# Block attention and its feed-forward: token chunks of 384 instead of 512, one PSUM bank moved, another pace of the half units

## The chip, the cores and the metric

One core of a Trainium2 chip runs the whole program in one launch. The metric is the device time of one execution in microseconds (us); lower is better. Its engines run side by side, each in the order of its own queue, and wait for each other on semaphores: TensorE (PE, with its weight loads shown as PEld) multiplies into PSUM, VectorE (DVE) and ScalarE (ACT) read PSUM and SBUF, GpSimd (POOL) works in SBUF, and SyncE (SP) issues every DMA of this kernel.

## What is computed

```python
# q, k, v: (8, 8, 576, 64) f32;  w_in: (512, 2048);  w_out: (2048, 512)
scores = np.matmul(q, k.transpose(0, 1, 3, 2)) / np.sqrt(64)
mask = block_i >= block_j                       # blocks of 64 positions
attn = exp(where(mask, scores, -1e9) - max)     # rows divided by their sum + 1e-9
x = np.matmul(attn, v)                          # (8, 8, 576, 64)
x = x.transpose(0, 2, 1, 3).reshape(4608, 512)  # heads side by side: 4608 tokens
h = x @ w_in
g = np.where(h >= 1, h, np.where(h <= -1, 0.0, (h + 1) ** 2 / 4))
out = g @ w_out                                 # (4608, 512) f32
```

## The kernel before

**Number format.** The products run in a rounded 32-bit format, with each operand held as a high and a low part, and three products of parts stand for one (high by high, low by high, high by low). The weights are taken apart on the chip: `prepare_weights` works through 64 pieces of 128 by 256, each with one DMA in, three DVE instructions, three on ACT and two on POOL. The parts of `w_in` stay in SBUF (`wih`, `wil`); those of `w_out` go to DRAM (`wo_split`) and come back 512 KB at a time.

**Attention.** A batch has four pairs of heads, so there are 32 pairs. `attention_steps` is a generator that lays out each pair in eight steps (a step ends at a `yield`), 258 steps in all: scores, softmax, transposes of the probabilities, products with `v`. From the second batch on, probabilities hop through a DMA (line 250) before they are transposed. Every result in PSUM takes a bank from `work_bank` (lines 80 to 85), which hands out the `ps_w` banks in turn; a bank comes free when ACT and DVE have read it. While `banks["free"]` holds, every second request gets a bank of `ps_o` instead.

**Feed-forward.** It goes by chunks of `TCH` = 512 tokens (9 chunks) and, in a chunk, by 16 slices of 128 hidden columns. One slice is one unit, made of two half units. `ffn_in` (lines 763 to 788) runs 12 matmuls of 512 columns into the one bank `ph`, then ACT L779, DVE L780 and DVE L783 turn it into `t` (L783 is the last to read `ph`), ACT L784 makes `gh`, POOL L785 `gl`, and SP L787 loads `wo`, of which there are two buffers. `ffn_out` (lines 790 to 811) runs 8 matmuls at L794 and 4 at L799, one set of 3 for each of the `NTT` = 4 groups of 128 tokens in the chunk, into 4 `po` banks; after the last slice the banks are copied out and stored. `feed_forward` yields after each half unit, and `ffn_out` of a slice comes behind `ffn_in` of the next.

**PSUM.** Eight banks: 3 `ps_w`, 1 `ph`, 4 `po` (lines 74 to 76).

**The interleaving** (lines 830 to 855). From step `START` = 36 (the fourth step of the fifth pair) one half unit of the feed-forward follows each attention step, and `want` sets how many weight pieces are converted by then: all 64 during the first 24 or so of these steps. When the attention has ended, the half units that are left run alone. The x of the attention goes to a ring of `RING` = 1536 tokens. The layout in the source is a priority; a scheduler at build time settles the order on each engine from its own estimates, so a few instructions stand earlier or later than their step.

## Time and profile before

| what | value |
| --- | --- |
| median of 3 runs | 1270.7 us (1269.4 to 1272.47) |
| the profiled execution: its time, its span | 1269.69 us, 1267.9 us |
| PE busy, share of the span | 1200.1 us, 95% |
| PEld, DVE, ACT, POOL busy | 998.8, 887.0, 703.2, 394.6 us |
| mean granted TensorE clock | 0.981 of full speed |
| matmuls | 6280, of which 3456 belong to the feed-forward |

The span is the time from the first to the last instruction of the profiled execution; the 1.8 us beside it lie around the program. Busy times of different engines overlap. Matmuls are pipelined and their ends are modelled, so the busy time of PE says little by itself: the distance from the start of one matmul to the start of the next is what a matmul takes in a stream. The trace falls into four stages, told apart by the steps of the source: attention with some weight pieces (steps 0 to 35, up to 113.6 us), attention with the rest of the weights and the first feed-forward half units (steps 36 to 67, 113.6 to 290 us, called the converting stage), attention with feed-forward (steps 68 to 257, 290 to 1081.9 us, the overlapped stage), and feed-forward alone (the tail, 1081.9 to 1268 us).

### The profile page before, as it was taken

The numbers are of one execution on the slowest core, as the hardware profiler recorded it, in microseconds if no ns is written. First come the engines' busy times: TensorE is split into PE (matmuls) and PEld (weight loads), VectorE is DVE, ScalarE is ACT, GpSimd is POOL, SyncE is SP. The second block draws the span as 40 slices with busy tenths as digits, with TensorE's granted clock in tenths as the row PEclk, the third lists the DMA queues.
The fourth block names the chain that finished last, engine by engine and source line by source line (L and its number), as shares of the span: only waits on it lengthen the run. The fifth ranks groups of instructions, "written<-read, shape, count | busy, mean of one in ns | idle before, by whom it ended". The sixth has DMA issues, their size and how long they took to land.

```text
span 1267.9 us, 20253 instructions
## 1 busy us (share of the span) xinstructions
PE 1200.1 (95%) x6280; PEld 998.8 (79%) x6280; DVE 887.0 (70%) x2188; ACT 703.2 (55%) x1827; POOL 394.6 (31%) x430
## 2 busy tenths in 40 slices
PE   5888889899999999999999999999999999999998
PEld 4666667678888888888888888888888888888886
DVE  8898877758777777777777777787777777322222
ACT  5787656646566655665656655566556555222222
POOL 3555655522222222222222222222222222222222
PEclk9888988999999999999999999999999999999999
DMA  5566666667888655555554655465556433422432
GB/s 158 167 176 215 203 228 197 217 198 237 260 273 266 215 162 158 154 175 163 156 162 145 187 157 152 138 189 153 160 154 190 137 128 118 132 87 98 133 100 100
DMA packets 185259, 215.43 MB, mean 170 GB/s; under 512 B 113840, under 2 KB 132272, under 8 KB 184384
## 3 DMA queue, kind: packets, MB, share of 16 engines
q1 hardware_dynamic: 185152, 214.14, 54.9%
q8 instruction: 50, 0.82, 0.3%
q14 instruction: 57, 0.47, 0.1%
HBM read 134.74 MB, written 31.98 MB: 131 GB/s over the span
## 4 chain that ended last, share of the span: by engine, by line
PE 69%; DVE 16%; ACT 6%; issue 5%; DMA 1%; POOL 1%; SPq 1%; ACTq 0%; POOLq 0%; DVEq 0%
PE ph L770 29%; PE po L794 15%; PE po L799 7%; PE ps_av L591 7%; PE ps_s L482 4%; ACT pr L509 3%; PE ps_s L485 3%; DVE t L780 2%; PE ps_t L552 2%; DVE t L783 2%; ACT t L779 2%; DVE pb L547 2%; DVE nm L505 2%; DVE sm L491 1%; DVE pr L515 1%
## 5 line engine op out<-in xcount | busy, mean ns | idle before, releaser
L785 POOL TENSOR_TENSOR gl<-t,gh 128x512 fp32r<-128x512 f32 x144 | 187.5, 1302 | 510.2 <-ACT gh L784 333.2
L794 PE MATMUL po<-wo,gh 128*128 128x512 f32 x1152 | 296.1, 397 | 0.5 <-DMA wo<-wo_split 0.3
L794 PEld LDWEIGHTS po<-wo,gh 128*128 128x128 f32 x1152 | 212.5, 189 | 44.5 <-DMA wo<-wo_split 0.7
L770 PE MATMUL ph<-xh,wih 128*128 128x512 f32 x576 | 232.9, 404 | 1.6 <-DVE t L783 1.6
L770 PE MATMUL ph<-xh,wil 128*128 128x512 f32 x576 | 228.8, 397 | 0.0
L770 PE MATMUL ph<-xl,wih 128*128 128x512 f32 x576 | 227.8, 396 | 0.5 <-DVE xl L627 0.5
L780 DVE SCALAR_TENSOR_TENSOR t<-t 128x512 f32<-128x512 f32 x144 | 101.5, 705 | 168.0 <-ACT t L779 165.2
L779 ACT ACTIVATE t<-ph 128x512 f32<-128x512 f32 x144 | 85.9, 597 | 173.8 <-PE ph L770 173.8
L509 ACT ACTIVATE pr<-ps_s,nm 128x128 f32<-128x128 f32 (+3 forms) x256 | 134.1, 527 | 60.5 <-DVE nm L505 58.4
L784 ACT CAST gh<-t 128x512 fp32r<-128x512 f32 x144 | 89.5, 621 | 120.3 <-DVE t L783 120.0
L799 PE MATMUL po<-wo,gl 128*128 128x512 f32 x576 | 155.6, 392 | 0.0
L482 PE MATMUL ps_s<-ka,qa 68*128 68x288 f32 (+4 forms) x384 | 135.3, 367 | 15.0 <-ACT pr L509 5.4
L379 POOL TENSOR_TENSOR vsr<-vn,vsr 128x256 fp32r<-128x256 f32 (+1 forms) x96 | 55.2, 576 | 246.2 <-ACT vsr L378 244.6
L770 PEld LDWEIGHTS ph<-xh,wil 128*128 128x128 f32 x576 | 109.5, 190 | 23.8
L770 PEld LDWEIGHTS ph<-xh,wih 128*128 128x128 f32 x576 | 109.8, 191 | 21.7 <-DVE t L783 2.3
L799 PEld LDWEIGHTS po<-wo,gl 128*128 128x128 f32 x576 | 108.7, 189 | 23.1
L505 DVE TENSOR_REDUCE nm<-ps_s 128x1 f32<-128x128 f32 (+3 forms) x256 | 118.8, 482 | 10.4 <-PE ps_s L485 9.4
L770 PEld LDWEIGHTS ph<-xl,wih 128*128 128x128 f32 x576 | 109.7, 190 | 20.5 <-DVE xl L627 0.9
L485 PE MATMUL ps_s<-kb,qb 128*128 128x288 f32 (+4 forms) x384 | 121.1, 322 | 0.0
L515 DVE TENSOR_SCALAR pr<-pr,sm 128x128 f32<-128x128 f32 (+3 forms) x256 | 107.3, 440 | 5.4
L783 DVE TENSOR_TENSOR t<-ph,t 128x512 f32<-128x512 f32 x144 | 98.7, 686 | 2.2
L491 DVE TENSOR_SCALAR sm<-sm 128x1 f32<-128x1 f32 (+1 forms) x224 | 52.0, 232 | 68.3 <-ACT pr L509 65.7
(111 smaller groups left out, 1871.4 us busy)
## 6 DMA issues: line engine op xcount, KB each, us to landing
wo<-wo_split SPq DMA_DIRECT2D x144, 512.0 KB, 3.5
prr<-pr SPq DMA_DIRECT2D x96, 192.0 KB, 2.5
prr<-pr SPq DMA_DIRECT2D x72, 256.0 KB, 2.8
out_dram<-ob SPq DMA_DIRECT2D x36, 256.0 KB, 2.9
bits<-in_moe_w_in_dram SPq DMA_DIRECT2D x32, 256.0 KB, 3.5
bits<-in_moe_w_out_dram SPq DMA_DIRECT2D x32, 256.0 KB, 3.0
wo_split<-ws SPq DMA_DIRECT2D x16, 512.0 KB, 2.9
qa<-qb SPq DMA_DIRECT2D x63, 128.0 KB, 2.4
```

The source lines that it names most:

```text
L482: nc.tensor.matmul(ps, qa[:KA, j, c0 : c0 + P], ka[:KA, j, k0 : k0 + n], start=first, stop=False)
L485: nc.tensor.matmul(ps, qb[:, j, c0 : c0 + P], kb[:, j, k0 : k0 + n], start=False, stop=last)
L505: nc.vector.tensor_reduce(out=nm[:, i : i + 1], in_=ps[:, cs], axis=AX.X, op=ALU.max, negate=True)
L509: nc.scalar.activation(pr[:, cs], ps[:, cs], AF.Exp, bias=nm[:, i : i + 1], scale=1.0, accum_out=sm[:, i : i + 1],)
L515: nc.vector.tensor_scalar_mul(pr[:, cs], pr[:, cs], sm[:, i : i + 1])
L770: nc.tensor.matmul(ph, w[:, cc, fs], x[:, cc, xs], start=(cc == 0 and i == 0), stop=(cc == NCC - 1 and i == 2),)
L779: nc.scalar.activation(t_, ph, AF.Relu, bias=0.5, scale=0.5)
L780: nc.vector.scalar_tensor_tensor(out=t_, in0=t_, scalar=1.0, in1=t_, op0=ALU.min, op1=ALU.mult)
L783: nc.vector.tensor_tensor(out=t_, in0=ph, in1=t_, op=ALU.max)
L785: nc.gpsimd.tensor_tensor(out=gl, in0=t_, in1=gh.bitcast(F32), op=ALU.subtract)
L794: nc.tensor.matmul(po[tt], gh[:, ts_], wo[:, w, :], start=(fc == 0 and w == 0), stop=False)
L799: nc.tensor.matmul(po[tt], gl[:, ts_], wo[:, 0, :], start=False, stop=fc == NFC - 1)
```

## The change

Chunks are 384 tokens: 12 chunks, `NTT` = 3, so that `po` takes three banks and `ps_w`, by `bufs=7 - NTT`, four. The matmuls of `ffn_in` have 384 columns instead of 512, and a unit has 12 of them as before; `ffn_out` has 9 matmuls of 512 columns instead of 12. The ring keeps 1536 tokens (4 chunks). Lines that used `TCH` as the width of a bank now use `BANK` = 512, with the same value as before. The pace: for the first 32 steps from `START` one half unit a step, as before, and then three half units for two steps (`due`). The number of weight pieces for each of these steps stays.

```diff
-    TCH = 512
+    TCH = 384
+    BANK = 512
...
-    RING = 3 * TCH
+    RING = 4 * TCH
...
-    ps_w = ctx.enter_context(tc.tile_pool(name="ps_w", bufs=3, space=bass.MemoryType.PSUM))
+    ps_w = ctx.enter_context(tc.tile_pool(name="ps_w", bufs=7 - NTT, space=bass.MemoryType.PSUM))
...
-            dst = pool.tile([P, TCH], F32R, tag=tag, name="prr")
+            dst = pool.tile([P, BANK], F32R, tag=tag, name="prr")
...
-        ph = ps_h.tile([P, 512], F32, tag="ph", name="ph")
+        ph = ps_h.tile([P, TCH], F32, tag="ph", name="ph")
...
-    converted = 0
+    converted = done = 0
...
         else:
+
+            due = i - START + 1 + max(0, i - START + 1 - 2 * NFC) // 2
             want = max(
-                EARLY + (i - START + 1) * (NFC // GROUP * PART - EARLY) // (2 * NFC - 4 * GROUP),
-                ((i - START) // (2 * GROUP) + 1) * PART,
+                EARLY + due * (NFC // GROUP * PART - EARLY) // (2 * NFC - 4 * GROUP),
+                ((due - 1) // (2 * GROUP) + 1) * PART,
             )
...
         if i >= START:
             banks["free"] = False
-            next(ffn_steps, None)
+            for _ in range(due - done):
+                next(ffn_steps, None)
+            done = due
```

## Rows read from the trace of the kernel before

**Rows 1.** Timeline, DVE: line 539 of the fifth and ninth pair (start, length).

```profile
113.76 0.16 DVE L539 TENSOR_TENSOR sm<-sm 128x1 f32<-128x1 f32 x1
...
289.54 0.16 DVE L539 TENSOR_TENSOR sm<-sm 128x1 f32<-128x1 f32 x1 [1.14 <-ACT pr L535]
```

**Rows 2.** Stretches: length, busy time by engine, granted clock, DMA share, GB/s.

```profile
113.60:290.00 176.40, 157.06 (x732) 122.71 (x733) 128.03 (x314) 102.93 (x289) 85.38 (x102) 0.92 0.67 212
290.00:1081.90 791.90, 777.78 (x4317) 659.32 (x4314) 608.88 (x1494) 473.63 (x1218) 209.17 (x218) 1.00 0.57 175
1081.90:1268.00 186.10, 180.90 (x796) 148.90 (x794) 49.68 (x73) 43.67 (x73) 43.99 (x34) 0.99 0.33 108
```

**Rows 3.** Waits of PE and PEld in the overlapped stage: total us, times, longest.

```profile
PE ps_qk L442 <- DVE x L614: 8.9, 23, 0.4
PE ps_s L482 <- ACT pr L509: 5.2, 17, 0.3
...
PEld ps_qk L442 <- PE ps_s L485: 15.7, 23, 0.7
PEld ps_s L482 <- ACT pr L509: 10.1, 23, 0.5
```

**Rows 4.** Timeline, one unit of the tail: start, length, engine, line.

```profile
1207.50 0.40 PE L770 MATMUL ph<-xh,wil 128*128 128x512 f32 x1
...
1207.73 1.98 PE L794 MATMUL po<-wo,gh 128*128 128x512 f32 x8
...
1209.35 0.69 DVE L783 TENSOR_TENSOR t<-ph,t 128x512 f32<-128x512 f32 x1
...
1210.46 0.39 PE L770 MATMUL ph<-xh,wih 128*128 128x512 f32 x1
```

**Rows 5.** Timeline, PE: a 384-column matmul and its successor.

```profile
728.78 0.34 PE L485 MATMUL ps_s<-kb,qb 128*128 128x384 f32 x1
728.96 0.39 PE L770 MATMUL ph<-xh,wih 128*128 128x512 f32 x1
```

**Rows 6.** Timeline, PE: the first two matmuls of a half unit behind attention.

```profile
712.91 0.47 PE L770 MATMUL ph<-xh,wih 128*128 128x512 f32 x1
...
713.22 0.39 PE L770 MATMUL ph<-xl,wih 128*128 128x512 f32 x1
```

**Rows 7.** Groups by line and shape: count, busy us, mean ns, idle before.

```profile
L779 ACT ACTIVATE t<-ph 128x512 f32<-128x512 f32 x144 | 85.9, 597 | 173.8 <-PE ph L770 173.8
...
L547 DVE TENSOR_TENSOR pb<-ps_t,pb 128x384 fp32r<-128x384 f32 x48 | 26.6, 554 | 0.7
...
L545 ACT CAST pb<-ps_t 128x384 fp32r<-128x384 f32 x48 | 22.8, 475 | 0.0
```

**Rows 8.** DMA issues of `wo`, and SP's waits in the overlapped stage.

```profile
wo<-wo_split SPq DMA_DIRECT2D x144, 512.0 KB, 3.5
...
SPq L787 <- PE ps_t L552: 169.3, 65, 6.4
```

**Rows 9.** Chain of waits in the converting stage: shares of its 176.4 us.

```profile
by line: PE ph L770 15.4%; issue 11.1%; PE ps_av L591 10.4%; POOL work L183 5.5%; PE po L794 4.6%; DVE t L780 3.4%; DVE work L177 3.1%; DVE work L171 3.0%; ACT pr L509 2.7%; DMA prs<-pr 2.5%; PE po L799 2.5%; DVE work L174 2.3%; DMA bits<-i
```

**Rows 10.** Converting stage, lines 770, 794 and 799 alone: length, PE, PEld, clock, DMA.

```profile
113.60:290.00 176.40, 56.65 (x192) 38.63 (x192) 0.92 0.67 212
...
113.60:290.00 176.40, 33.97 (x120) 22.67 (x120) 0.92 0.67 212
...
113.60:290.00 176.40, 16.97 (x60) 11.83 (x60) 0.92 0.67 212
```

**Rows 11.** Waits of PE in the converting stage for banks that scores hold.

```profile
PE ps_av L591 <- ACT pr L509: 3.7, 3, 2.2
PE ps_t L552 <- ACT pr L509: 3.0, 2, 1.9
```

**Rows 12.** Timeline, PE: two neighbours in a slow stretch of the converting stage.

```profile
117.16 0.63 PE L770 MATMUL ph<-xl,wih 128*128 128x512 f32 x1
117.58 0.63 PE L770 MATMUL ph<-xh,wil 128*128 128x512 f32 x1
```

More of the change, by code (lines that the diff above doesn't have):

```diff
@@ L234, in as_float32r @@
                 spare["of"] = [t_[:, :NTL, :, :].rearrange("p t h d -> p (t h d)") for t_ in vsr]
-                spare["of"].append(att1.tile([P, S], F32R, tag="x32", name="prs")[:, :TCH])
+                spare["of"].append(att1.tile([P, S], F32R, tag="x32", name="prs")[:, :BANK])
                 spare["end"] = att1.tile([P, G0 + P], F32R, tag="pa11", name="pre")[:, :BLK]
@@ L238, in as_float32r @@
             spare["n"] += 1
-            if src.shape[1] > TCH:
+            if src.shape[1] > BANK:
                 moved.append(spare["end"])
             for i, dst in enumerate(moved):
-                n = min(TCH, src.shape[1] - i * TCH)
-                nc.sync.dma_start(dst[:, :n].bitcast(F32), src[:, i * TCH : i * TCH + n])
+                n = min(BANK, src.shape[1] - i * BANK)
+                nc.sync.dma_start(dst[:, :n].bitcast(F32), src[:, i * BANK : i * BANK + n])
             return moved
         moved = []
-        for c0 in range(0, src.shape[1], TCH):
-            n = min(TCH, src.shape[1] - c0)
+        for c0 in range(0, src.shape[1], BANK):
+            n = min(BANK, src.shape[1] - c0)
             pool, tag = ((conv, "bits"), (conv2, "work"))[c0 > 0]
-            dst = pool.tile([P, TCH], F32R, tag=tag, name="prr")
+            dst = pool.tile([P, BANK], F32R, tag=tag, name="prr")
             nc.sync.dma_start(dst[:, :n].bitcast(F32), src[:, c0 : c0 + n])
@@ L549, in transposed @@
         def transposed(self, out, parts, c0, n):
-            src = parts[c0 // TCH][:, c0 % TCH : c0 % TCH + n] if self.hop else parts[0][:, c0 : c0 + n]
+            src = parts[c0 // BANK][:, c0 % BANK : c0 % BANK + n] if self.hop else parts[0][:, c0 : c0 + n]
             if self.hop:
```

## The prediction

> **What bounds the kernel now.** The page comes first: PE is busy 95% of the span, but its matmul ends are modelled, so the next question is where PE stands still. The busy times by stretch answer it. I cut the trace where the fourth step of the fifth and of the ninth pair ends (line 539 runs once a pair) [rows 1], because the source starts the feed-forward at the first and has converted all weights by the second. In the overlapped stage PE is busy 777.8 of 791.9 us at full clock; in the tail all but the start and the end [rows 2]. So both are bound by PE, and DVE, the next, has 608.9 us to do there. In the converting stage PE is busy 157.1 of 176.4 us at a clock of 0.92, DVE 128.0 [rows 2], and the chain of waits runs over PE, DVE, POOL and DMA by turns [rows 9]: no engine bounds it alone.
>
> The view of the waits says what PE's 14.1 idle us in the overlapped stage are: 8.9 before L442 and 5.2 before L482 [rows 3]. Both are waits for a bank. L442 (`turned_last`) needs the bank that `attn_v_first` took three requests earlier, which DVE L614 empties; the 512-column scores need the one whose exponentials (ACT L509) end late. The weight loads show the same waits as 15.7 and 10.1 us [rows 3], longer because modelled matmul ends cover part of them.
>
> **The change, part by part.** *A matmul.* [...] A half unit of either kind costs 2.73 us now. Afterwards `ffn_in` costs 12 x 0.174 = 2.09 and `ffn_out` 9 x 0.2275 = 2.05.
>
> [...]
>
> *Where the half units lie.* The converting stage has 32 steps, the overlapped one 190. Half units in them and in the tail, before: 32 (17 `ffn_in`), 190, 66. After: 32, 285 (222 + 95 = 317 by the last step), 67. PE time:
> - converting: 87.4 before; 17 x 2.09 + 15 x 2.05 = 66.3 after: -21.1.
> - overlapped: 518.7 before; 142 x 2.09 + 143 x 2.05 = 590.0 after: +71.3.
> - tail: 180.2 before; 33 x 2.09 + 34 x 2.05 = 138.7 after: -41.5.
>
> Together +8.7: the kernel gets no less matmul work, it gets it at other places. In the tail and the overlapped stage, where PE is the bound, these are times. In the converting stage -21.1 is only an offer.
>
> *The fourth bank.* With it L442 needs the bank of the scores before, whose exponentials come two requests earlier, and the 512-column scores that of an earlier transpose. So the two waits go: 14.1 us by the idle time, 25.8 by the loads [rows 3]. I take -18, nearer to the idle time, as the transposes behind them then wait for probabilities instead, now and then. The scheduler's other choices could take all of it (bound 0).
>
> *Starts.* A half unit that begins behind attention has 0.31 from its first to its second matmul [rows 6], 0.08 over the pitch. The 95 half units more are 47 units more: +3.8 (0 to 4).
>
> *The single `ph` bank.* `ffn_in` waits until L783 has read `ph`. In the tail this is 1207.50 to 1210.04, 2.54 us from the start of the last matmul, and the next `ffn_in` starts at 1210.46 [rows 4]. At 384 columns ACT's part shrinks from 597 to about 475 ns and DVE's two from 0.69 to about 0.55 each [rows 4, 7], the last matmul by 0.05: 2.54 - 0.12 - 0.27 - 0.05 = 2.10, and PE is back after 0.17 + 2.05 = 2.22. The margin falls from 0.42 to 0.12, so the first load may come late: +1 in the tail (0 to 5). In the overlapped stage two in three `ffn_in` will have but one attention step between them, the shortest with five transposes and two 512-column matmuls, at least 0.7 us by their streams: 2.9 against 2.1 plus what ACT and DVE do in between. I take +1 (0 to 20).
>
> *Other engines.* 48 units more of five instructions on ACT, DVE and POOL are shorter each; DVE's two make 192 x 1.10 = 211 against 200 us, covered by its idle 183 us in the overlapped stage. The `wo` loads go from 144 to 192. Each waits on SP for a buffer, and the DMA hops of the probabilities queue behind it; SP stands there 169 us of 792 [rows 8]. A buffer's turn, in the tail 2.09 + 2.05 + 2.09 = 6.2 us, still covers the 3.5 to landing, so I take nothing; if that cover went, a hop would be late and a transpose would wait as in the third rival. Before step 36 the banks are still seven, so nothing moves.
>
> *The converting stage.* What does it give back of 21.1? At least what leaves the chain: L770 15.4%, L794 and L799 7.1%, L780 3.4% of 176.4 us [rows 9], times 0.234, 0.25 and 0.20: 6.4 + 3.1 + 1.2 = 11. At most what leaves PE's busy time, where a part runs at 1.2 GHz: 56.65 x 0.234 + 50.94 x 0.25 = 26 [rows 10], and the waits for score banks, 6.7 [rows 11]: 33. I take -21: PE is busy 89% of the stage, which draws to the upper end, and the pieces' chain over DVE and POOL, unchanged, to the lower.
>
> *Sum.* Overlapped +71.3 - 18 + 3.8 + 1 = +58.1; tail -41.5 + 1 = -40.5; converting -21. Together -3.4 on the span of 1267.9, so 1264.5, and with the 1.8 us around it 1266.3. The profiled run lies 1.0 under the median, so 1267 for the median.
>
> **The rivals.** *The converting stage does not give it back* (slower). The balance of the other stages is +17.6, so below 17.6 the change loses. For it: the weight pieces keep their number a step, and POOL and DVE work on them stands in the chain beside 11.1% "issue" [rows 9]. A PE with less to do may also run slower: neighbours at 117.16 are 0.42 apart, 1.2 GHz, and the stage's clock is 0.92 [rows 2, 12]. Against: the feed-forward's own lines hold 26% of that chain. With 6 to 10 us given back: 1278 to 1282.
>
> [...]
>
> *The converting stage is PE's* (faster): 33 back, and 20 or more for the banks: 1250 to 1257. For it: 89% busy. Against: DVE, 5 us lighter, would be busy 86% of the 143 us left.
>
> *`ph` becomes the wait.* If the chain L779, L780, L783 takes over 2.9 us because attention stands in ACT's and DVE's queues, 95 of the 142 `ffn_in` wait, by 0.2 us 19 us: 1286. Against: two steps' slack is gone only for two in three.
>
> *The waits stay* (the change does not do what it says): the bank was not the last condition, only the latest semaphore. The 18 us are not gained: 1285. Against: L442 reads `qk`, which the source loads six steps earlier.
>
> *Weight loads bind at 384 columns*: 148.90 us for 794 loads in the tail [rows 2], 0.19 each, against 0.174: 2304 x 0.016 = 37 us, 1304. Against: [rows 5].
>
> **How the numbers follow.** Chances: forecast 0.42 (its own range 1260 to 1274), no giving back 0.23, PE's stage 0.17, `ph` 0.09, waits stay 0.06, loads 0.03. The range 1250 to 1284 leaves out a third of PE's stage, half of the two cases at 1285 and the loads, 0.16 in all. A measurement here can tell about 0.2%, 2.5 us, from no change. Faster by more: 0.27 of the forecast's 0.42 and all of PE's stage, 0.44. Within: 0.12 of the forecast and the upper edge of no giving back, 0.17. Slower: the rest, 0.39.
>
> **What would show it.** In the trace after: 384-column neighbours at L770 0.174 apart (0.19: loads); no wait before L442 and L482 in the overlapped stage; that stage at some 850 us, the tail at 146, the converting stage at 155. A converting stage over 160 us makes the forecast wrong; a wait of L770 on L783 there or in the tail points to `ph`.

## The result, and the profile after

The changed kernel takes 1273.49 us (median of 20 runs, 1270.51 to 1276.81) against 1267.99 for the kernel before, timed beside it (20 runs): a ratio of 1.0044, with a 95% interval of 1.0034 to 1.0054. It is slower by more than the 0.2% that can be told apart, where I had forecast 1267 and a gain as the likeliest. The profiled execution has a span of 1271.5 us; that of before had 1267.9, a difference of 3.6. The medians lie 5.5 apart; most of the rest is that the profiled execution of before, 1269.69 us, lies 1.7 above the median of its 20 runs.

The stretches of the changed kernel, cut at the same events as [rows 1] (line 539 is now 540): length, busy time and count of PE, PEld, DVE, ACT and POOL, granted clock, DMA share, GB/s.

```profile
0.00:113.10 113.10, 83.89 (x443) 68.30 (x444) 99.77 (x311) 82.93 (x250) 56.00 (x76) 0.92 0.58 172
113.10:281.20 168.10, 134.53 (x699) 111.77 (x698) 123.18 (x313) 100.78 (x289) 80.19 (x102) 0.94 0.69 216
281.20:1125.40 844.20, 842.26 (x5015) 766.91 (x5014) 659.54 (x1595) 493.82 (x1309) 229.60 (x266) 1.00 0.63 196
1125.40:1271.50 146.10, 141.15 (x706) 124.03 (x704) 41.32 (x73) 35.79 (x71) 35.38 (x35) 1.00 0.41 135
```

Cut at exactly those events, the stages of before [rows 1, 2] are 113.8, 175.7, 792.4 and 186.0 us; its converting stage, so cut:

```profile
113.80:289.50 175.70, 156.36 (x730) 122.10 (x730) 127.45 (x310) 102.72 (x287) 85.38 (x102) 0.92 0.66 211
```

| stage | before | after | change | forecast |
| --- | --- | --- | --- | --- |
| first (steps 0 to 35) | 113.8 | 113.1 | -0.7 | 0 |
| converting | 175.7 | 168.1 | -7.6 | -21 |
| overlapped | 792.4 | 844.2 | +51.8 | +58.1 |
| tail | 186.0 | 146.1 | -39.9 | -40.5 |
| span | 1267.9 | 1271.5 | +3.6 | -3.4 |

**The overlapped stage and the tail came nearly as worked out.** The waits of PE and PEld in the overlapped stage (total, times, longest) answer [rows 3]:

```profile
PE po L795 <- DMA wo<-wo_split: 0.9, 1, 0.9
PE ph L771 <- DVE t L784: 0.9, 4, 0.3
...
PEld ph L771 <- DVE t L784: 10.8, 31, 0.7
```

The waits before L442 and L482 (now 443 and 483) are gone; PE is busy 842.26 of 844.20 us. A unit of the tail answers [rows 4] (start, length, engine, line):

```profile
1201.51 0.33 PE L771 MATMUL ph<-xl,wih 128*128 128x384 f32 x1
...
1203.24 0.34 PE L771 MATMUL ph<-xh,wil 128*128 128x384 f32 x1
...
1203.41 1.55 PE L795 MATMUL po<-wo,gh 128*128 128x512 f32 x6
...
1204.79 0.56 DVE L784 TENSOR_TENSOR t<-ph,t 128x384 f32<-128x384 f32 x1
...
1205.48 0.37 PE L771 MATMUL ph<-xh,wih 128*128 128x384 f32 x1
```

From 1201.51 to 1203.41 lie eleven distances of 384-column matmuls, 0.173 each (0.174 had been worked out). From the start of the last one to the end of L784, which frees `ph`, pass 2.11 us, and PE is back 2.24 us after that start: the forecast had 2.10 and 2.22. The first load of the next `ffn_in` waits a moment in 32 units (6.3 us in all), the matmuls themselves don't.

**The converting stage is where the forecast failed.** PE's busy time there, cut at the same events, was 156.36 us before and is 134.53 now, 21.8 less, about the 21.1 that the half units had promised. But its idle time went from 19.3 to 33.6. What PE waits for now (first fence), and what ACT and DVE wait for (second):

```profile
PE ph L771 <- DVE t L784: 17.4, 8, 4.4
PE ps_t L553 <- DMA prs<-pr: 6.5, 5, 1.8
PE ps_t L553 <- DMA vsr<-pr: 2.9, 6, 0.9
```

```profile
ACT wih L186 <- POOL work L184: 20.3, 16, 3.2
...
ACT ws L186 <- POOL work L184: 9.4, 11, 1.5
...
DVE t L781 <- ACT t L780: 11.8, 8, 2.5
```

The waits for score banks of [rows 11] are not among PE's larger ones any more. In their place PE stands 17.4 us at `ffn_in`, because `ph` is not free: L781 waits 11.8 us for ACT's L780, and ACT in its turn stands 29.7 us at the copy of a weight piece (L186), which needs POOL's addition (L184). That stop of ACT is not new: in the kernel before it was 27.1 us (15.4 and 11.7). What is new is that PE, with less to do, reaches `ph` before it is free (1.6 us of such waits before). The transposes wait for probabilities that hop through a DMA. The chain of waits of this stage, to be held against [rows 9]:

```profile
by line: issue 12.6%; POOL work L184 6.8%; DMA prs<-pr 5.8%; PE ph L771 4.3%; DVE work L172 4.1%; DVE work L178 4.0%; PE ps_av L592 3.7%; DVE pr L516 3.6%; DVE work L175 3.6%; DMA prr<-pr 3.5%; PE po L795 3.0%; ACT pr L510 2.9%; DVE t L781 
```

L770's share was 15.4%, that of L794 and L799 7.1%; now L771 has 4.3% and L795 3.0%. POOL's and DVE's lines of the pieces (L184, L172, L178, L175) add up to 18.5%, and "issue" and two hops of probabilities to 21.9%. Most of the feed-forward's matmuls left the chain, and the chain became only a little shorter. By pairs, the four of the stage took 39.5, 46.7, 49.1 and 40.4 us before, and 33.2, 40.3, 50.1 and 44.6 after: the first two gave back 12.7 us, the last two took 5.2 of it again.

### The profile page after: what moved, and what is told of

It reads as the page before. It is cut to its first block, busy times and chain, and to the rows that moved or that the text cites. A ratio compares the mean times of both kernels' runs of the same rounds, so it can differ in the third digit from the quotient of the medians.

```text
span 1271.5 us, 21767 instructions
## 1 busy us (share of the span) xinstructions
PE 1201.8 (95%) x6856; PEld 1071.0 (84%) x6856; DVE 923.8 (73%) x2290; ACT 713.3 (56%) x1917; POOL 401.2 (32%) x478
## 4 chain that ended last, share of the span: by engine, by line
PE 77%; DVE 11%; DMA 3%; ACT 3%; issue 2%; POOL 1%; SPq 1%; DVEq 0%; ACTq 0%; POOLq 0%
PE ph L771 29%; PE po L795 19%; PE po L800 9%; PE ps_av L592 7%; PE ps_s L483 4%; PE ps_t L553 3%; PE ps_s L486 3%; DVE pr L516 2%; DVE nm L506 1%; PE ps_qk L402 1%; DVE work L172 1%; DVE t L781 1%; DVE work L175 1%; POOL work L184 1%; ACT pr L510 1%
## 5 line engine op out<-in xcount | busy, mean ns | idle before, releaser
L786 POOL TENSOR_TENSOR gl<-t,gh 128x384 fp32r<-128x384 f32 x192 | 195.6, 1019 | 655.0 <-ACT gh L785 478.5
L795 PE MATMUL po<-wo,gh 128*128 128x512 f32 x1152 | 305.7, 399 | 2.5 <-DMA wo<-wo_split 2.2
L771 PE MATMUL ph<-xh,wih 128*128 128x384 f32 x768 | 267.7, 349 | 19.5 <-DVE t L784 18.4
L771 PE MATMUL ph<-xh,wil 128*128 128x384 f32 x768 | 259.9, 338 | 0.0
L771 PE MATMUL ph<-xl,wih 128*128 128x384 f32 x768 | 259.4, 338 | 0.0
L781 DVE SCALAR_TENSOR_TENSOR t<-t 128x384 f32<-128x384 f32 x192 | 130.0, 677 | 152.5 <-ACT t L780 148.7
L795 PEld LDWEIGHTS po<-wo,gh 128*128 128x128 f32 x1152 | 208.6, 189 | 38.1 <-DMA wo<-wo_split 1.7
L785 ACT CAST gh<-t 128x384 fp32r<-128x384 f32 x192 | 98.6, 513 | 207.6 <-DVE t L784 206.5
L771 PEld LDWEIGHTS ph<-xh,wih 128*128 128x128 f32 x768 | 145.6, 190 | 42.6 <-DVE t L784 37.3
L780 ACT ACTIVATE t<-ph 128x384 f32<-128x384 f32 x192 | 94.0, 490 | 135.1 <-PE ph L771 133.7
L800 PE MATMUL po<-wo,gl 128*128 128x512 f32 x576 | 164.1, 392 | 0.0
L771 PEld LDWEIGHTS ph<-xl,wih 128*128 128x128 f32 x768 | 145.6, 190 | 3.0
L771 PEld LDWEIGHTS ph<-xh,wil 128*128 128x128 f32 x768 | 145.3, 189 | 0.2
L506 DVE TENSOR_REDUCE nm<-ps_s 128x1 f32<-128x128 f32 (+3 forms) x256 | 119.0, 484 | 21.8 <-PE ps_s L486 20.8
L800 PEld LDWEIGHTS po<-wo,gl 128*128 128x128 f32 x576 | 108.2, 188 | 23.5
L784 DVE TENSOR_TENSOR t<-ph,t 128x384 f32<-128x384 f32 x192 | 105.8, 551 | 2.3
L553 PEld LDWEIGHTS ps_t<-ident_r,prr 128*128 128x128 f32 x600 | 68.9, 139 | 14.6 <-ACT t L780 1.5
L548 DVE TENSOR_TENSOR pb<-ps_t,pb 128x512 fp32r<-128x512 f32 (+1 forms) x120 | 76.0, 634 | 3.3 <-ACT pb L546 1.8
```

Source lines behind the costliest of these rows:

```text
L506: nc.vector.tensor_reduce(out=nm[:, i : i + 1], in_=ps[:, cs], axis=AX.X, op=ALU.max, negate=True)
L553: nc.tensor.transpose(out.bitcast(F32R), src, ident_r)
L771: nc.tensor.matmul(ph, w[:, cc, fs], x[:, cc, xs], start=(cc == 0 and i == 0), stop=(cc == NCC - 1 and i == 2),)
L781: nc.vector.scalar_tensor_tensor(out=t_, in0=t_, scalar=1.0, in1=t_, op0=ALU.min, op1=ALU.mult)
L784: nc.vector.tensor_tensor(out=t_, in0=ph, in1=t_, op=ALU.max)
L786: nc.gpsimd.tensor_tensor(out=gl, in0=t_, in1=gh.bitcast(F32), op=ALU.subtract)
```

## The experiments

The question of the first runs: are the weight pieces what holds the converting stage, and by which engine; and is the fourth bank, or `ph`, what the change is worth elsewhere? All stage lengths below are cut at the same events as above, and in each run the stages that the edit doesn't touch came out within 3 us of the kernel that it starts from, unless the text says so. A stage length comes from one profiled execution, and in the converting stage the granted clock lay anywhere from 0.86 to 0.99 in these runs, so a few us there say little by themselves. Where a kernel was run four times or more, an estimate from its median helps: the median less the 1.8 us around the span and less the overlapped stage and the tail of its trace leaves the first two stages together, 287.8 us before and 281.4 after, 6.4 apart. The kernels of 4, 5 and 7 and the first two of 6 were run once each.

**1. Pieces without DVE's work.** The three DVE instructions are left out, POOL adds to what ACT wrote (the same edit in both kernels).

```diff
-        nc.vector.tensor_scalar(out=top, in0=top, scalar1=F32_TOP, ...)
-        nc.vector.tensor_scalar(out=mag, in0=top.bitcast(U32), scalar1=3, ...)
-        nc.vector.scalar_tensor_tensor(out=mag, in0=top.bitcast(U32), ...)
...
-        nc.gpsimd.tensor_tensor(out=w32, in0=w32, in1=low, op=ALU.add)
+        nc.gpsimd.tensor_tensor(out=w32, in0=top.bitcast(I32), in1=low, op=ALU.add)
```

> The kernel before, but each of the 64 weight pieces leaves out its three DVE instructions (clamp, shift, sign), 85 us of DVE in all, so that the weights hold other values; everything else stays. Theory A: the weight pieces pace the converting stage (175.7 us before, 168.1 us after the change), and PE time taken out of it comes back only in part. By A this kernel's converting stage falls towards PE's own work there, 155 to 162 us, and with the first stage, which has 24 of the pieces, the total falls to 1235 to 1250. Theory B: the stage is paced by PE and by its waits for attention and for the ph bank; then it stays at 170 to 176 and the total falls by under 15 us.

> The changed kernel with the same three DVE instructions left out of each weight piece (weights hold other values). It is compared with e1_light_before. Theory A: without the pieces' DVE work the converting stage is PE's, so the 21 us of feed-forward that the change takes out of it come back almost in full: converting stage 137 to 145 us, 15 to 21 under e1_light_before, and the total 5 to 14 us below e1_light_before (the sign of the change turns). Theory B (PE's waits for ph, L784, and for the hops of the probabilities eat the gain): converting stage within 10 us of e1_light_before, total 0 to 6 us above it.

Measured: 1246.99 us for the kernel before with the edit (ratio to before 0.984, 0.981 to 0.986), 1257.91 for the changed one (0.992, 0.989 to 0.995). Most of that is the first stage (99.3 and 100.7 us). The converting stage went from 175.7 to 165.1 in the kernel before and only from 168.1 to 167.5 in the changed one. By the medians the first two stages together are 266.8 and 265.5 us, 1.3 apart where it was 6.4. So DVE's part of the pieces is not what hides the changed kernel's gain: without it the two kernels come no further apart. My first theory, that DVE binds the stage once PE is lighter, fell here (it had 137 to 145 us for the changed kernel's stage; for the kernel before neither theory had 165). That the changed kernel's stage even lies 2.4 us above the other is not to be read as a loss: the traced executions lie 2.5 us below and 2.7 above their medians, the stage's clock is 0.97 in the one and 0.90 in the other, and in the changed kernel PE is busy 140.1 us, more than the 134.5 with DVE's work. How much of 10.6 against 0.6 is the clock stays open.

**2. The size of the first chunk.** The chunk that runs in the converting stage gets 512 or 256 tokens, and the second chunk makes up for it (256 or 512); the others stay as in the change. The second kernel begins with `[256, 512]` in the same place. The fourth `po` bank of a 512 chunk is borrowed from the attention's four.

```diff
-    NCH = NT // TCH
+    SIZES = [512, 256] + [TCH] * 10
+    STARTS = [sum(SIZES[:c]) for c in range(len(SIZES))]
+    NCH = len(SIZES)
```

> The changed kernel with chunks of 512, 256 and then ten of 384 tokens: the first chunk, which lies in the converting stage, has the size of before, and its fourth po bank is one of the four work banks for that time; from the second chunk on four work banks as in the change. The feed-forward in the converting stage is 87.4 us of PE again and the later stages have 21.1 us less than in the change. Theory A (that stage hides PE work): converting stage 172 to 178 us, overlapped stage 844 - 21 = 823, tail 146, total 1256 to 1262, below both kernels. Theory B (PE's work costs its time wherever it lies): within 4 us of the changed kernel, 1268 to 1276.

> The same with chunks of 256, 512 and ten of 384: the converting stage has 45 us of feed-forward on PE, 21 less than in the change, and the overlapped stage 21 more. Theory A: the converting stage gives back at most 6 us more, 160 to 168, overlapped 865, total 1284 to 1292. Theory B: 1268 to 1276 as for the change.

Measured: 1265.61 us (ratio to before 0.9989, 0.9976 to 1.0003) with 512 first, 1290.76 (1.0177, 1.0156 to 1.0198) with 256 first. By the pitches of the traces (0.2275 us for 512 columns [rows 4], 0.173 for 384 as above, and 0.119 for 256, eleven distances from 304.60 to 305.91 in the trace of the 512-first kernel) the feed-forward of the stage is an estimated 87, 66 and 45 us of PE for 512, 384 and 256 tokens; the stage took 171.4, 168.1 and 164.9. So 21 us of PE work more or less move it by 3.2 or 3.3. The medians agree: the first two stages together are 284.6, 281.4 and 276.7 us, 3.2 and 4.7 apart. Work put into this stage is nearly free, and work taken out of it brings nearly nothing. In the overlapped stage the same steps cost more: 832.8, 844.2 and 865.9 us, 11.4 and 21.7. That is the trade of the change: 21 us of PE work were moved from where they cost some 3 us to where they cost 11 to 22. The 11.4 was a miss, for I had expected a full 21 (823 us, and 1256 to 1262 for the whole); the kernel with 512 first is only level with before.

With 256 first part of what was taken out went into slower matmuls:

```profile
111.60:276.50 164.90, 124.58 (x642) 102.03 (x643) 118.33 (x313) 97.90 (x289) 76.67 (x102) 0.86 0.69 217
```

The granted clock of the stage is 0.86 where it was 0.94 with 512 and with 384, and PE's busy time fell by 10.0 us (134.5 to 124.6), not by 21; its idle time rose from 33.6 to 40.3.

**3. The fourth bank and the single `ph`.** One kernel leaves the eighth bank unused (the line of `ps_w` alone), the other gives it to `ph` (both lines).

```diff
-    ps_w = ctx.enter_context(tc.tile_pool(name="ps_w", bufs=7 - NTT, ...))
-    ps_h = ctx.enter_context(tc.tile_pool(name="ps_h", bufs=1, ...))
+    ps_w = ctx.enter_context(tc.tile_pool(name="ps_w", bufs=6 - NTT, ...))
+    ps_h = ctx.enter_context(tc.tile_pool(name="ps_h", bufs=2, ...))
```

> The changed kernel with three work banks, the eighth bank unused: the chunk size and the pace alone. If the fourth bank is what ended the waits of L442 and of the 512-column scores, they return, and the overlapped stage is 14 to 26 us longer than the 844.2 of the changed kernel (858 to 870), the tail stays at 146, the total is 1286 to 1300. If the larger share of feed-forward between attention steps ended them, the overlapped stage stays within 5 us of 844. The converting stage tells whether PE's waits for score banks come back there beside the waits for ph: 168 to 176.

> The changed kernel with three work banks and two ph banks: the fourth bank goes to ph. Theory P (the single ph bank eats the gain of the converting stage: L771 waited 17.4 us for L784 there): those waits go and the converting stage falls to 150 to 160. Theory Q (PE runs ahead of DVE, ACT and POOL there and stops at whatever buffer they still hold): the stage stays at 163 to 173, with other waits of PE in the place of those. The overlapped stage is as with three work banks, 855 to 870, in both.

Measured: 1311.62 us (ratio 1.0348, 1.0331 to 1.0366) and 1307.08 (1.0306, 1.0287 to 1.0324). The overlapped stage is 877.7 and 876.0 us, the converting stage 171.4 and 172.8. The three-bank kernel's overlapped stage (the stretch, then two waits of PE):

```profile
284.50:1162.20 877.70, 853.14 (x5017) 769.56 (x5015) 658.93 (x1595) 502.77 (x1308) 229.59 (x266) 1.00 0.61 188
...
PE ps_s L483 <- ACT pr L510: 17.0, 46, 0.8
PE ps_qk L443 <- DVE x L615: 7.0, 21, 0.3
```

The two bank waits of [rows 3], 14.1 us before, are 24.0 here; the waits of the weight loads for the same banks are 40.3 (25.9 and 14.4). The fourth bank takes them away and 33.5 us with them, more than the 14 to 26 that I had expected. And a second `ph` bank changes little in the converting stage: PE's waits at `ph` there fall from 12.4 us only to 9.0, and the stage is 172.8 against 171.4 (the first two stages by the medians 283.9 against 286.1). So, with three banks at least, the waits at `ph` are where PE happens to stand, not what holds the stage; four banks together with a second `ph` were not run. In the overlapped stage PE waits 0.9 us at `ph`. With that the rival "`ph` becomes the wait" is out.

**4. All pieces ahead of the feed-forward.** All 64 pieces are laid out before step 36.

```diff
-    EARLY = 24
+    EARLY = 64
```

> The changed kernel with all 64 weight pieces laid before the first feed-forward half unit (EARLY = 64 instead of 24), so that the converting stage has attention and feed-forward alone and the first stage is 50 to 80 us longer. Compared with e8_early_before. Theory C1 (the pieces on DVE, ACT, POOL and SP together make the converting stage hide PE work): without them the stage is PE's, 118 to 132 us here, 16 to 21 under e8_early_before, and this kernel's total is 3 to 12 below that one's. Theory C2 (the attention's own chain from scores to hop in this batch hides it): the stage is under 12 us shorter than that of e8_early_before, and the total above it.

> The kernel before with the same EARLY = 64. C1: converting stage 136 to 150 us, and its length less that of e7_early_after is 16 to 21. C2: under 12. The overlapped stage and the tail stay at 792 and 186 in both.

Measured: 1303.39 and 1305.52 us. The first stage grows to 170.4 and 170.8, the converting stage shrinks to 138.4 and 154.5. Its stretches, for the changed kernel and for the one before:

```profile
170.40:308.80 138.40, 124.76 (x692) 108.21 (x692) 80.00 (x222) 71.66 (x197) 34.41 (x42) 0.94 0.70 213
```

```profile
170.80:325.30 154.50, 143.09 (x721) 116.87 (x722) 84.42 (x220) 75.72 (x197) 38.42 (x42) 0.96 0.74 230
```

Now the difference is 16.1 us where it was 7.6, and the changed kernel is the faster one, by 2.1. So it is the pieces, whatever they do, that hide PE's saving. (Each of the two was run once; the 2.1 us alone would not carry this, the 16.1 in the stage do.) The difference is the 16 to 21 of theory C1; both stages are longer than it had, by 6.4 and 4.5 us, and the gain of the whole is less than its 3 to 12.

**5. More buffers for the pieces.** Six buffers instead of three; to make room the low parts of `w_in` are written over the high ones.

```diff
-    conv = ctx.enter_context(tc.tile_pool(name="conv", bufs=3))
-    conv2 = ctx.enter_context(tc.tile_pool(name="conv2", bufs=3))
+    conv = ctx.enter_context(tc.tile_pool(name="conv", bufs=6))
+    conv2 = ctx.enter_context(tc.tile_pool(name="conv2", bufs=6))
...
-    wil = const.tile([P, NCC, DF], F32R, tag="wil", name="wil")
+    wil = wih
```

> The changed kernel with six buffers instead of three in each of the two pools of the weight pieces (conv and conv2); the room comes from putting the low parts of w_in over the high parts (one tile for both), so the output differs, while every instruction stays. Theory D: a piece goes through DMA, ACT, DVE, POOL, ACT and POOL, each a queue of its own, and holds its two buffers for that time, so with three buffers the pieces come at the rate of their latency, and attention and feed-forward wait in the same queues behind them. With six the converting stage falls to 140 to 158 us. Theory E (the shared in-order queues alone set it, not the buffers): 162 to 172. The overlapped stage and the tail stay at 844 and 146.

> The kernel before with the same six buffers and the same shared tile. Theory D: converting stage 156 to 168 us, 12 to 21 more than e9_buffers_after. Theory E: 168 to 178, 5 to 10 more than e9_buffers_after. Overlapped 792, tail 186 in both.

Measured: the stage took 169.1 and 174.1 us, the whole 1279.53 and 1268.19. The difference is 5.0, as theory E had it. It is not the number of these buffers that limits how fast a piece goes through. (The stage's clock was 0.87 and 0.95, so the 5.0 itself is rough.) The two buffers of the tag `wo`, which the pieces of `w_out` share with the loads of `wo`, stayed two.

**6. POOL's addition, and ACT's stop behind it.** First the addition of the low part is left out.

```diff
         w32 = mag.bitcast(I32)
-        nc.gpsimd.tensor_tensor(out=w32, in0=w32, in1=low, op=ALU.add)
         w32 = w32.bitcast(F32)
         nc.scalar.copy(hi(), w32)
```

> The changed kernel with weight pieces that leave out POOL's addition of the low part (L184), so that ACT's copy behind it no longer waits for POOL: the weights have other values, the rest of the work stays. In the changed kernel ACT stands 29.7 us of the converting stage at that copy (20.3 and 9.4 us in the view of the waits). Theory F, this stop of ACT is what the stage is late by, since L780 and the exponentials stand behind it in ACT's queue: the stage falls from 168.1 to 145 to 157 us, and the difference to the kernel before with the same pieces rises from 7.6 to 14 to 21 us. Rival G, no single stop does it, the pieces' work as a whole and the attention's own latency do: the stage stays at 160 to 170, the difference at 5 to 10.

> The kernel before with weight pieces that leave out POOL's addition of the low part (L183): the weights have other values. There ACT stands 27.1 us of the converting stage at the copy. Theory F: the stage, 175.7 us, falls to 164 to 171, less than in the changed kernel, because PE's own work then bounds it. Rival G: 168 to 176.

Measured: 1259.03 us for the changed kernel and 1252.38 for the one before; the stage 154.6 and 160.6. The changed kernel's stretch:

```profile
111.10:265.70 154.60, 133.43 (x700) 110.55 (x699) 113.12 (x310) 99.16 (x285) 53.58 (x65) 0.94 0.72 227
```

POOL is busy 26.6 us less than in the changed kernel, and the stage is 13.5 us shorter. But the kernel before gained 15.1 from the same edit. The addition is a large part of what this stage costs, in both kernels alike, and the difference is 6.0: by these single runs it is not what hides the gain. Theory F had the changed kernel's stage right and its main point, the difference, wrong; the 160.6 of the kernel before lies below what either theory gave.

Then the addition stays, and ACT's copy is laid out one piece later, so that POOL has had time for it.

```diff
         w32 = w32.bitcast(F32)
+        yield
         nc.scalar.copy(hi(), w32)
...
-    LAG = 2
+    LAG = 3
```

> The kernel before, with all its work, in which ACT's copy of a weight piece (L184) is laid out one piece later than POOL's addition that it waits for, instead of right behind it. If ACT's stop at POOL is the 15 us that the run without the addition gained in the converting stage (175.7 to 160.6): the stage falls to 160 to 170 us, the whole by 5 to 15. If what that run gained was POOL's time (27 us less busy) and not ACT's stop: the stage stays at 172 to 178.

> The changed kernel with the same later copy (L186). If ACT's stop is what the run without the addition gained (168.1 to 154.6): the converting stage falls to 153 to 163 us, the whole by 5 to 15, and the difference to the kernel before with the same edit stays at 5 to 9. If it was POOL's time: 165 to 170.

Measured: 1270.09 us for the changed kernel (ratio to before 1.0018, 1.0006 to 1.0031) and 1269.24 for the one before (1.0011, 0.9997 to 1.0025). The stage fell to 159.4 and 171.1, by 8.7 and 4.6, while the first stage, where pieces run too, rose by 4.2 and 3.9. The changed kernel's stretch, and ACT's waits in it:

```profile
117.30:276.70 159.40, 136.35 (x693) 113.68 (x694) 118.45 (x308) 99.73 (x286) 79.39 (x99) 0.90 0.70 222
...
ACT wih L187 <- POOL work L184: 10.9, 9, 1.7
ACT ws L187 <- POOL work L184: 9.0, 10, 1.7
```

ACT's stop went from 29.7 to 19.9 us, with POOL's work unchanged. So part of what the addition costs is ACT's stop. About half of the changed kernel's gain in this stage, and nearly all of the other's, is lost in the first stage, so the changed kernel gets 3.4 us faster and the other not at all, where 5 to 15 had been expected. The difference in the stage rose to 11.7, above the expected 5 to 9, and the medians of the two kernels are 0.9 us apart instead of 5.5: by them the first two stages are 289.1 and 276.8 us, 12.3 apart where it was 6.4. So the place of this copy seems to hide some 6 us of PE's saving, though without the addition, where ACT's copy cannot wait for it either, the difference did not grow; why not stays open. The later copy from step 36 on alone was not tried.

**7. Pieces without a chain over the engines, and without loads.** A piece is reduced to its load and two ACT instructions (it has three); then, in the changed kernel alone, the load is replaced by three blocks that are loaded once.

```diff
-        nc.scalar.mul(top, bits[:, :, 1].bitcast(F32), 2.0**-112)
-        nc.scalar.mul(low, low.bitcast(U32), 2.0**-29)
...
-        nc.gpsimd.tensor_tensor(out=w32, in0=w32, in1=low, op=ALU.add)
-        w32 = w32.bitcast(F32)
-        nc.scalar.copy(hi(), w32)
+        nc.scalar.copy(hi(), bits[:, :, 1].bitcast(F32))
         yield
-        nc.gpsimd.tensor_tensor(out=lo(), in0=w32, in1=hi().bitcast(F32), op=ALU.subtract)
+        nc.scalar.mul(lo(), bits[:, :, 0].bitcast(U32), 2.0**-29)
```

and for the last kernel also

```diff
-        bits = conv.tile([P, CW, 2], I32, tag="bits", name="bits")
-        nc.sync.dma_start(bits, source.bitcast(I32).rearrange("p (n t) -> p n t", t=2))
+        if n < 3:
+            kept.append(conv.tile([P, CW, 2], I32, tag="bits", name="bits"))
+            nc.sync.dma_start(kept[n], source.bitcast(I32).rearrange("p (n t) -> p n t", t=2))
+        bits = kept[n % 3]
```

> The changed kernel with weight pieces that consist of the DMA in and two ACT instructions only, with no DVE and no POOL work and four ACT instructions fewer in no case: the weights have other values. It takes the pieces' chain over the engines away and leaves their DMAs, their issues on SP and most of ACT's time. If the chain ACT, DVE, POOL, ACT, POOL of a piece standing in the in-order queues is the cause: the converting stage falls from 168.1 to 138 to 148 us (138.4 is what it took with all pieces ahead of it), and the difference to the kernel before with the same pieces is 14 to 21 us. If the DMAs and SP's queue are the cause: the stage stays at 158 or more, the difference under 12.

> The kernel before with weight pieces that consist of the DMA in and two ACT instructions only: the weights have other values. If the chain of a piece over the engines is the cause: the converting stage falls from 175.7 to 154 to 164 us (154.5 is what it took with all pieces ahead of it), less than the changed kernel's. If the DMAs and SP's queue are the cause: 165 or more.

> The changed kernel with weight pieces that consist of two ACT instructions only, on three blocks of weights that are loaded once: beside DVE's and POOL's work the 256 KB load of each piece is left out (the weights have other values; the stores to wo_split stay). With the loads the stage took 153.5 us at a DMA share of 0.77, with all pieces ahead of it 138.4 at 0.70. If the loads and their place in SP's queue are the last cover: the converting stage falls to 138 to 145 us, 11 to 18 below the 156.1 of the kernel before without DVE and POOL work, a kernel that stands within 2 us of its own 154.5 already. If ACT's two instructions a piece or the stores are it: it stays at 150 or more.

Measured: 1245.46 us for the changed kernel with the loads, 1230.48 for the one before, 1217.06 for the changed one without loads. The stage: 153.5, 156.1 and 126.3. The changed kernel with the loads (stretch, chain, two waits of PE), where line numbers are lower by 24:

```profile
99.70:253.20 153.50, 130.18 (x693) 108.88 (x692) 72.17 (x205) 90.59 (x255) 22.55 (x28) 0.96 0.77 242
...
by line: DMA wo<-wo_split 12.5%; DMA wo_split<-ws 9.0%; PE ps_av L568 8.8%; PE po L771 7.9%; PE ph L747 5.3%; DMA bits<-in_moe_w_out_dram 3.6%; PE po L776 3.2%; SPq L278 2.5%; SPq L274 2.4%; PE ps_s L459 1.7%; issue 1.6%; PE ps_t L529 1.4%;
...
PE ph L747 <- DVE t L760: 11.6, 8, 2.2
PE po L771 <- DMA wo<-wo_split: 8.6, 5, 3.0
```

and without them, with line numbers lower by 20:

```profile
97.10:223.40 126.30, 120.02 (x682) 103.71 (x681) 68.40 (x202) 78.40 (x220) 22.38 (x28) 0.99 0.73 228
...
by line: PE ph L751 19.8%; PE ps_av L572 18.6%; PE po L775 14.5%; DMA wo<-wo_split 8.1%; PE po L780 7.2%; PE ps_t L533 5.0%; PE ps_s L463 4.6%; PE ps_s L466 4.3%; DMA wo_split<-ws 4.1%; DMA prs<-pr 3.3%; DMA vsr<-pr 2.4%; PE ps_qk L403 2.0%
```

With the loads, the kernel before came down to 156.1, within 2 us of its time without pieces, as the theory of the chain had it for that kernel. The changed one did not: 153.5, neither the 138 to 148 of the one theory nor the 158 of the other. Its chain now goes over the stores of the converted `w_out` to DRAM and their way back into `wo` (21.5%), and PE waits 8.6 us for `wo`. Without the loads, 27.2 us go, more than I had expected: PE is busy 120.02 of 126.30 us at a clock of 0.99, the chain is PE's (L751, L572, L775 and L780 have 60%), and no wait for `ph` is left among its larger ones. This is a stage bound by PE. The kernel before was not run this way, so what the change would give back there was not measured.

**8. A version with another pace.** The 512-first kernel of 2, with one half unit a step for 32 steps, then two a step for 16, then four for three steps up to the 96th, then three for two.

```diff
-            due = i - START + 1 + max(0, i - START + 1 - 2 * NFC) // 2
+            n = i - START + 1
+            if n <= 32:
+                due = n
+            elif n <= 48:
+                due = 32 + 2 * (n - 32)
+            elif n <= 96:
+                due = 64 + (n - 48) * 4 // 3
+            else:
+                due = 128 + (n - 96) * 3 // 2
```

> e5_first512 (chunks of 512, 256 and ten of 384) with another pace behind the converting stage: two half units a step while the chunk of 256 runs, then four for three steps until step 131, then three for two. In e5_first512 the pairs over the chunk of 256 took 30.7, 30.0 and 32.5 us where PE's work is some 28, so PE waited there. If the thin half units are the reason, the overlapped stage falls from 832.8 to 822 to 828 and the total to 1254 to 1261, below both kernels. If the converting stage's delay moves on, it stays within 3 us of e5_first512 (1262 to 1269).

Measured: 1265.74 us, 0.9983 of the kernel before (0.9971 to 0.9995). The stages are 114.1, 172.5, 833.7 and 146.0: the pace gave the overlapped stage nothing over the 832.8 of the 512-first kernel. That is within 3 us of the 512-first kernel, as the second expectation had it. By its ratio it is the lowest of the kernels that do all the work, but 0.17% is less than the 0.2% that can be told apart, and the interval overlaps that of the 512-first kernel without the pace.

## Why the prediction failed, by its own steps

**The step that failed is "The converting stage ... I take -21".** The converting stage by what its pieces do, each length from one trace:

| pieces | before | after | difference |
| --- | --- | --- | --- |
| as they are | 175.7 | 168.1 | 7.6 |
| no DVE work | 165.1 | 167.5 | -2.4 |
| six buffers | 174.1 | 169.1 | 5.0 |
| no addition on POOL | 160.6 | 154.6 | 6.0 |
| copy a piece later | 171.1 | 159.4 | 11.7 |
| load and two ACT instructions | 156.1 | 153.5 | 2.6 |
| all ahead of the stage | 154.5 | 138.4 | 16.1 |
| two ACT instructions, no load | not run | 126.3 | |

It came to -7.6. I had drawn the value to the upper end because "PE is busy 89% of the stage". The busy time did fall by 21.8, but a busy share of 89% is made of pieces of work that wait for each other in turn. The chain of before already said so: its feed-forward lines held 26% [rows 9], and the rest was DVE, POOL, DMA and "issue". The lower bound that came from that chain, 11 us, was itself too high, because taking the feed-forward off the chain let other waits, which had run beside it, take its place. The two rows of the chain show that: 22.5% for L770, L794 and L799 before, 8.1% for L771, L795 and L800 now (0.8% of it L800), with the stage only 7.6 us shorter.

What is shown: the stage hides PE work, for 21 us of it move the stage by some 3 us (2); it is the pieces that hide it, for with them out of the stage the two kernels are 16.1 us apart there (4); and the changed kernel's stage becomes PE's when their engine chain and their loads are gone (7). No single one of the suspected causes does all of it: not DVE's work, not the buffers, not `ph`, not the addition. ACT's stop at the copy is a part, some 6 us by the medians (6). What is left open is how the loads and stores hold the stage: by their place in SP's queue, by the DMA engines' time (a share of 0.77 with the loads, 0.73 without), by the length of the way load, ACT, store, `wo`, or by the two buffers that `ws` of the pieces and `wo` of the feed-forward share. The kernel before without loads, which would give the last difference, was not run. SP's queue is a rival of its own that no run tests. SP issues every DMA of this kernel in order, also the loads of `wo` and the hops of the probabilities (in this stage's batch at L244, and L243 in the kernel before; the line 250 named for them serves the later batches). In the changed kernel's converting stage it stands at the store of a piece of `w_out` and at the load of the next piece (total, times, longest):

```profile
SPq L214 <- POOL ws L188: 16.4, 9, 2.7
SPq L165 <- POOL work L184: 15.3, 11, 3.3
```

That is 31.7 us, and 32.0 (11.4 and 20.6) in the kernel before; with six buffers the store alone still has 17.7. Issuing the pieces' DMAs from another queue was not tried.

In the converting stage PE had the highest busy share before (0.89), and 21.8 us less of it were worth 7.6: read as a price of the work, the share does not hold here.

**The overlapped stage.** Without the fourth bank it grew by 85.3 us (792.4 to 877.7), of which 71.3 are the half units' PE time as worked out; 14 are other costs where I had 4.8. PE's idle time explains 9.9 of the 14 by the two bank waits (14.1 to 24.0), which leaves 4.1 for the starts and the rest. The bank itself brought 33.5 where I had taken 18; my argument for staying near the idle time undervalued it. The 33.5 lie between the 24.0 of PE's idle time and the 40.3 of the loads' waits with three banks, and above the 14.1 and 25.8 of [rows 3], from which I had worked. Both terms were mis-sized and in opposite directions: +14 - 33.5 = -19.5 where the forecast had -18 + 3.8 + 1 = -13.2. The waits went, as the forecast said, so "the waits stay" is out, and with pitches of 0.173 "weight loads bind" too. The 0.174 us of a 384-column matmul was an estimate, and no run shows the division of a pitch on which it stood. What the runs show are the pitches: 0.2275 us at 512 columns, 0.173 at 384 and 0.119 at 256 (2), so about 0.054 for 128 columns more. The 0.7 us of the shortest attention step was an estimate too: in the trace of before five transposes in a row take 0.35 us (431.14 to 431.49), and with two pitches of 0.2275 that makes 0.8.

**The tail** came to -39.9 where -40.5 was worked out, and `ph` as forecast, 2.11 against 2.10.

**The rival that came true** is "the converting stage does not give it back", with 6 to 10 us, on the other side of the forecast. Its condition was that the change loses below the balance of the other stages. That balance was +11.2 instead of 17.6 (51.8 - 39.9 - 0.7), because the bank brought more, so the loss is 3.6 on the span and not the 8 to 12 of that rival. "The converting stage is PE's" needed what only the run without the pieces' engine work and loads shows. The slow clock in which I had seen a reason for it had no part between these two traces: the stage's clock is 0.94, against 0.92 before. The 1.2 GHz named for it is an estimate, 512 columns by the 0.42 us of [rows 12]; the clock granted there is 0.50 of full speed (115.05 to 118.00 us in the trace of before), and the pitch 0.426 (seven distances from 115.03 to 118.01). With 256 tokens first, where PE has 21 us less to do again, the stage's clock fell to 0.86 (2). That the lighter PE is the cause was not shown: with six buffers, and the work of the changed kernel, it was 0.87 (5).

**That the whole came near the number is luck.** Of the 7.0 us by which the span missed, the converting stage made +13.4, the other costs of the overlapped stage +9.2, the tail +0.6, the bank -15.5 and the first stage -0.7. Two misses one way and one the other nearly cancelled, and the sign of the change still came out wrong.

## What to carry to other kernels

The busy share of the busiest engine in a stage where several in-order queues feed each other was no price here: before work is moved out of such a stage, vary the amount of it there (one chunk larger, one smaller) and read the slope, here some 3 us for 21. Work moved out of a stage that has a cover for it into one that is bound cost 11 to 22 us for 21 here, so fill the covered stage first. And the price of a PSUM bank, 33.5 us, lay here above PE's idle time for it (24.0) and below the waits of the weight loads (40.3).

## What the runs showed of the hardware that I had not expected

DVE's `scalar_tensor_tensor` L781 (two inputs from SBUF) hardly got shorter on the mean, from 705 to 677 ns. Groups by line and shape, over the whole span (count, busy us, mean ns, idle before):

```profile
L781 DVE SCALAR_TENSOR_TENSOR t<-t 128x384 f32<-128x384 f32 x192 | 130.0, 677 | 152.5 <-ACT t L780 148.7
...
L784 DVE TENSOR_TENSOR t<-ph,t 128x384 f32<-128x384 f32 x192 | 105.8, 551 | 2.3
L785 ACT CAST gh<-t 128x384 fp32r<-128x384 f32 x192 | 98.6, 513 | 207.6 <-DVE t L784 206.5 <-PE po L795 0.8
L780 ACT ACTIVATE t<-ph 128x384 f32<-128x384 f32 x192 | 94.0, 490 | 135.1 <-PE ph L771 133.7 <-POOL gl L786 0.5 <-PE ps_t L553 0.2
```

L784, L785 and L780 fell from 686, 621 and 597 ns (the last of them in [rows 7]) to 551, 513 and 490, while L781 has 677. Its single instances explain it (timeline, POOL and DVE; then the line's minimum, median and maximum in the overlapped stage):

```profile
631.62 1.55 POOL L658 TENSOR_TENSOR xl<-x,xh 128x576 fp32r<-128x576 f32 x1 [0.23 <-ACT xh L657]
...
631.97 1.62 DVE L781 SCALAR_TENSOR_TENSOR t<-t 128x384 f32<-128x384 f32 x1
...
638.52 0.55 DVE L781 SCALAR_TENSOR_TENSOR t<-t 128x384 f32<-128x384 f32 x1
...
L781 DVE SCALAR_TENSOR_TENSOR t<-t x142: 546/558/1631, 287.9 to 1123.0; 128x384 f32<-128x384 f32 x142
```

In the overlapped stage L781 takes 0.55 us, except where POOL's L658 is running: then it ends some 0.4 us after POOL's instruction. All 22 of 142 that run over 0.8 us (1.11 to 1.63) overlap an L658, and no shorter one overlaps an instruction of lines 658, 786 or 380 on POOL. Of the two in the fence, the one beside L658 took 1.62 us and the other 0.55. In the kernel before the same line had a mean of 691 ns in the overlapped stage and 692 in the tail, and none of its instances there overlaps a POOL instruction. It costs DVE some 20 us in the changed kernel (22 times about 0.9), beside a PE that is busy nearly all the time, and PE's waits for DVE there are 0.9 us. In the converting stage, where POOL works on the pieces, L781 has a median of 0.758 us, and the same line 0.550 in the run whose pieces have no POOL work and no loads.
